# Six heads' decay masks from one interleaved table of powers, read in one transfer ahead of the second pair's q

## The chip, the cores and the metric

The kernel runs on one core of a Trainium2 chip. The metric is device time in microseconds (us). Three runs of the kernel before took 605.57, 605.16 and 603.69 us; their median is 605.16 us.

## What is computed

Three blocks follow each other: a linear attention whose weights decay with distance, a token- and channel-mixing MLP, and a two-dimensional Fourier mixing with a second MLP. The change lies in the first block. Batch is 2, with 8 heads, 768 positions and 64 values a head, all in float32. The decay of head h is the number `lam[h]`, between 0.97 and 0.99.

```python
rel = pos[:, None] - pos[None, :]
Dmask = np.where(rel >= 0, lam[:, None, None] ** rel[None, :, :], 0.0)
lam_pow = lam[:, None, None] ** (pos[None, :, None] + 1)
...
intra = np.einsum('bhic,bhjc->bhij', qb, kb) * Dmask[None]
intra = np.einsum('bhij,bhjd->bhid', intra, vb)
inter = np.einsum('bhid,bhde->bhie', qb * lam_pow[None], kv_state)
out[:, :, sl] = intra + inter
```

## The kernel before, in words

The kernel cuts the sequence into NC = 6 blocks of C = 128 positions and takes the heads two at a time: a pair (b, hp) is batch b and heads 2hp and 2hp + 1. There are eight pairs, numbered 0 to 7 as 4b + hp.

For each pair, `load_kp` (L400) brings the transposed keys into one of four slots of the tile `kp`, and `load_qkv` (L394) brings q, and then k and v in one transfer, into a tile `qkv`. `attention_scores` multiplies keys with queries on TensorE (L417). VectorE multiplies the scores by the head's decay mask on their way out of PSUM (L420: for each head one multiply of 4 blocks, 512 elements, and one of 2 blocks, 256 elements). GpSimd scales q by the powers of the decay (L424). `attention_states` scales the keys on ScalarE (L438, with the last column of the mask), forms the block updates on TensorE (L444) and chains them on VectorE (L448, L450). `attention_out` copies the states on ScalarE (L462), and TensorE adds both parts of the result (L468, L471), which ScalarE copies to `xT` (L473).

The masks lie in the tile `att` as `dT`, one 128 x 128 square per head. Each is a Toeplitz square: row p is a row of powers, shifted by p places. `attention_setup` makes them in two ways.

Heads 0 and 1 (the near heads, for pairs 0 and 4) are built on VectorE from the identity `ident` by seven doubling steps (L359, L374); the powers of lam that these steps need come from GpSimd (L371), from `lam_bc`, a copy of lam on all partitions.

Heads 2 to 7 (the far heads) come by way of memory. `pw8` has one head per partition and 256 places: 127 zeros, a one, and 128 powers, made by seven doubling multiplies on VectorE (L341). SP writes it to `scratch` in device memory (L344). The function `skew` (L348) reads it back, 128 rows per head, each one float further on than the last. `skew(2, 6)` stands behind pair 1's loads and fetches four heads, `skew(6, H)` stands behind pair 2's loads and fetches two (L1027).

GpSimd clears `bd` in `att` (L361), and makes the powers `pw` that scale q (L388) once the near masks are built.

The orders of SP and TensorE are written out by hand, in the order of the calls; those of VectorE, ScalarE and GpSimd come from a scheduler. The string `EARLY` (L37) gives the order of the front part: s for scores, u for states, r for the result of a pair, w for 8 warm-up transposes, l for loads, c and d for conversions of weights, x, h and o for the token mixing. 22 warm-up transposes (L1048) stand ahead of it; they read `ident`. The conversions turn 64-bit words into floats on ScalarE and VectorE (L231, L254 to L259); a raw weight tile can be loaded only once an earlier one has been converted, and SP issues in order. So raw_a_0, the first weight tile of the channel MLP, and behind it pair 7's loads, go out when VectorE has finished the last word operation (L259) of a token-mixing tile.

Of the kernel before, what the change touches and what calls it, by code (L numbers as in the profile page):

```python
# [25 lines left out]
P = 128  # L26
C = 128
# [35 lines left out]
def body(ctx: ExitStack, tc: tile.TileContext, qkv, kT, lam, w_tok1, w_tok2,  # L63
# [259 lines left out]
    def attention_setup():  # L323

        pw8 = temp(2 * C, "pw8")[:H]
        nc.sync.dma_start(pw8[:, C:C + 1], lam.rearrange("(h o) -> h o", o=1))
        lam_bc = sm_p.tile([P, H], F32, name="lam_bc")
        nc.scalar.dma_start(lam_bc, lam.rearrange("(o h) -> o h", o=1).broadcast_to([P, H]))
        kp = big_tile("kp").rearrange("p (i s) -> p i s", i=4)[:, :, :S]
        kps = [kp[:, i, :].rearrange("p (c j) -> p c j", j=C) for i in range(4)]  # L330
        load_kp(0, 0, kps[0])
        t = half_tile([P, 4, S], "qkv_0_0")
        for i in range(3):
            nc.sync.dma_start(t[:, i, :], qkv[0, 0, :, i])
        load_kp(0, 1, kps[1])
        nc.vector.memset(pw8[:, 0:C - 1], 0.0)
        nc.vector.memset(pw8[:, C - 1:C], 1.0)
        n = 1
        while n < C:
            w = min(n, C - n)  # L340
            ts(out=pw8[:, C + n:C + n + w], in0=pw8[:, C:C + w], scalar1=pw8[:, C + n - 1:C + n], scalar2=None,  # L341
               op0=ALU.mult)
            n *= 2
        nc.sync.dma_start(scratch, pw8)  # L344
        att = big_tile("att")
        dT = att[:, 0:H * C].rearrange("p (h j) -> p h j", h=H)

        def skew(h0, h1):  # L348
            src = bass.AP(scratch.tensor, scratch.offset + h0 * 2 * C, [[1, P], [2 * C, h1 - h0], [1, C]])
            nc.sync.dma_start(dT[:, h0:h1, :], src)  # L350

        load_qkv(0, 1)
        skew(2, 6)

# [9 lines left out]
        while n < C:  # L364
# [7 lines left out]
            for h in range(2):  # L372
                src = bands[i % 2][:, h]
                built = stt(out=dT[:, h, :] if 2 * n == C else bands[1 - i % 2][:, h, C // 2:],  # L374
                            in0=src[:, C // 2 - n:C // 2 - n + C], scalar=by[:, h:h + 1], in1=src[:, C // 2:],
                            op0=ALU.mult, op1=ALU.add).ins
# [15 lines left out]
        return dT, pw, kps, [bd[:, i] for i in range(2)], skew  # L392

    def load_qkv(b, hp):  # L394
        t = half_tile([P, 4, S], f"qkv_{b}_{hp}")
        nc.sync.dma_start(t[:, 0, :], qkv[b, hp, :, 0])
# [8 lines left out]
    def attention_scores(b, hp, dT, pw, kp):  # L405
# [5 lines left out]
        for g, cs in enumerate((range(4), range(4, NC))):  # L411
# [6 lines left out]
            for a in range(2):  # L418
                st = st2[:, a] if g else temp(4 * C, f"st_{n}_{a}").rearrange("p (c j) -> p c j", c=4)
                tt(out=st, in0=ps[a][:, :m * C].rearrange("p (c j) -> p c j", c=m),  # L420
                   in1=dT[:, 2 * hp + a:2 * hp + a + 1, :].to_broadcast([P, m, C]), op=ALU.mult)
# [7 lines left out]
    def attention_states(b, hp, dT, pw):  # L429
# [6 lines left out]
        with tc.issue_after(on_act[behind]):  # L436
            for a in range(2):
                on_act["keys", NP * b + hp] = nc.scalar.activation(  # L438
                    kn[:, :NC - 1, a * D:(a + 1) * D], kn[:, :NC - 1, a * D:(a + 1) * D], AF.Copy,
                    scale=dT[:, 2 * hp + a, C - 1:C]).ins  # L440
# [578 lines left out]
    with tc.manual_schedule(engines={ENG.SP, ENG.PE}):  # L1019
        dT, pw, kps, bds, skew = attention_setup()  # L1020
# [6 lines left out]
        skew(6, H)  # L1027
# [178 lines left out]
```

## Time and profile before

| what | value |
|---|---|
| median of three runs | 605.16 us |
| profiled execution | 605.05 us |
| its span | 603.1 us |
| TensorE matmul busy | 585.0 us, 97% |
| VectorE busy | 410.4 us, 68% |
| ScalarE busy | 269.9 us, 45% |
| GpSimd busy | 138.8 us, 23% |
| mean transfer rate | 109 GB/s |

The profiled execution is one run of the program; its span reaches from the first to the last instruction, and 1.95 us lie around it. Busy times are averages over stages with different limits, so a stage is read by itself: `PE` is TensorE's matmul, `PEld` its weight load, `DVE` VectorE, `ACT` ScalarE, `POOL` GpSimd, `SP` the engine that issues most transfers, and a q behind an engine's name its instruction queue. In a row of the timeline the bracket at the end gives the idle time just before it and what ended that wait.

### The profile page before, as it was taken

The numbers are of one execution on the slowest core, as the hardware profiler recorded it, in microseconds if no ns is written. First come the engines' busy times: TensorE is split into PE (matmuls) and PEld (weight loads), VectorE is DVE, ScalarE is ACT, GpSimd is POOL, SyncE is SP. The second block draws the span as 40 slices with busy tenths as digits, with TensorE's granted clock in tenths as the row PEclk, the third lists the DMA queues.
The fourth block names the chain that finished last, engine by engine and source line by source line (L and its number), as shares of the span: only waits on it lengthen the run. The fifth ranks groups of instructions, "written<-read, shape, count | busy, mean of one in ns | idle before, by whom it ended". The sixth has DMA issues, their size and how long they took to land. (4 is left out here: it accounts for less than half of the span.)

```text
span 603.1 us, 9588 instructions
## 1 busy us (share of the span) xinstructions
PE 585.0 (97%) x3704; PEld 545.9 (91%) x3704; DVE 410.4 (68%) x768; ACT 269.9 (45%) x536; POOL 138.8 (23%) x119
## 2 busy tenths in 40 slices
PE   8789999999999999999999999999999999999997
PEld 7777899999999999999989899899899888999886
DVE  6788893474586656848796896768775765664435
ACT  2756981255475555534454451324533434431110
POOL 5252331023230041101364110013501213120000
PEclk9999999999999999999999999999999999999999
DMA  7964431014448767410232000002521232200005
GB/s 275 407 261 158 185 122 60 0 71 141 137 148 265 245 192 219 146 64 2 57 101 71 19 2 35 18 1 58 168 88 36 88 122 88 87 2 1 0 1 209
DMA packets 24637, 65.58 MB, mean 109 GB/s; under 512 B 2824, under 2 KB 3984, under 8 KB 24592
## 3 DMA queue, kind: packets, MB, share of 16 engines
q1 hardware_dynamic: 24304, 64.83, 32.1%
q8 instruction: 29, 0.48, 0.3%
q10 hardware_dynamic: 288, 0.14, 0.1%
q14 instruction: 16, 0.13, 0.1%
HBM read 54.99 MB, written 9.97 MB: 108 GB/s over the span
## 5 line engine op out<-in xcount | busy, mean ns | idle before, releaser
L526 DVE SCALAR_TENSOR_TENSOR hid<-ph,hid 128x384 fp32r<-128x384 f32 x68 | 37.6, 553 | 59.6 <-ACT hid L525 59.4
L145 PE MATMUL ac<-w_b,hid 128*128 128x512 f32 x192 | 75.8, 395 | 0.0
L144 PE MATMUL ac<-w_b,hid 128*128 128x512 f32 x192 | 75.7, 394 | 0.0
L143 PE MATMUL ac<-w_b,hid 128*128 128x512 f32 x192 | 74.9, 390 | 0.0
L143 PE MATMUL ph<-uh,w_a 128*128 128x384 f32 x192 | 64.7, 337 | 0.0
L143 PE MATMUL ac<-hid,w_b 128*128 128x384 f32 x192 | 64.5, 336 | 0.0
L144 PE MATMUL ac<-hid,w_b 128*128 128x384 f32 x192 | 64.3, 335 | 0.0
L145 PE MATMUL ph<-uh,w_a 128*128 128x384 f32 x192 | 64.2, 335 | 0.0
L145 PE MATMUL ac<-hid,w_b 128*128 128x384 f32 x192 | 64.2, 334 | 0.0
L144 PE MATMUL ph<-uh,w_a 128*128 128x384 f32 x192 | 64.2, 334 | 0.0
L525 ACT ACTIVATE hid<-ph 128x384 fp32r<-128x384 f32 x68 | 33.1, 487 | 69.3 <-PE ph L145 68.9
L287 POOL TENSOR_TENSOR w_a<-m_a,w_a 128x512 fp32r<-128x512 f32 x18 | 25.5, 1418 | 131.9 <-ACT w_a L286 131.9
L145 PEld LDWEIGHTS ac<-w_b,hid 128*128 128x128 f32 x192 | 36.0, 188 | 7.7
L144 PEld LDWEIGHTS ac<-w_b,hid 128*128 128x128 f32 x192 | 36.0, 188 | 6.1
L143 PEld LDWEIGHTS ac<-w_b,hid 128*128 128x128 f32 x192 | 36.1, 188 | 5.8
L287 POOL TENSOR_TENSOR w_b<-m_b,w_b 128x512 fp32r<-128x512 f32 x18 | 25.3, 1403 | 49.6 <-ACT w_b L286 32.4
L143 PEld LDWEIGHTS ph<-uh,w_a 128*128 128x128 f32 x192 | 36.1, 188 | 0.4 <-issue 0.2
L144 PEld LDWEIGHTS ac<-hid,w_b 128*128 128x128 f32 x192 | 36.1, 188 | 0.3 <-DVE hid L526 0.3
L144 PEld LDWEIGHTS ph<-uh,w_a 128*128 128x128 f32 x192 | 36.1, 188 | 0.1
L143 PEld LDWEIGHTS ac<-hid,w_b 128*128 128x128 f32 x192 | 36.1, 188 | 0.0
L145 PEld LDWEIGHTS ph<-uh,w_a 128*128 128x128 f32 x192 | 36.0, 188 | 0.0
L145 PEld LDWEIGHTS ac<-hid,w_b 128*128 128x128 f32 x192 | 36.0, 188 | 0.0
(504 smaller groups left out, 1467.0 us busy)
## 6 DMA issues: line engine op xcount, KB each, us to landing
qkv<-qkv SPq DMA_DIRECT2D x7, 768.0 KB, 10.0
single_scratch<-m_a SPq DMA_DIRECT2D x16, 256.0 KB, 4.4
qkv<-qkv SPq DMA_DIRECT2D x10, 384.0 KB, 5.9
kp<-kT SPq DMA_DIRECT2D x8, 384.0 KB, 6.9
out<-u SPq DMA_DIRECT2D x11, 256.0 KB, 2.1
single_scratch<-m_b SPq DMA_DIRECT2D x10, 256.0 KB, 5.3
raw_t_0d<-w_tok SPq DMA_DIRECT2D x2, 384.0 KB, 9.3
raw_t_1d<-w_tok SPq DMA_DIRECT2D x2, 384.0 KB, 2.9
```

The lines of the kernel that those rows point to most:

```text
L143: nc.tensor.matmul(ps, wt[0], xt[0], start=first, stop=False, **kw)
L144: nc.tensor.matmul(ps, wt[0], xt[1], start=False, stop=False, **kw)
L145: nc.tensor.matmul(ps, wt[1], xt[0], start=False, stop=last, **kw)
L287: nc.gpsimd.tensor_tensor(out=t[:, 1, :n], in0=src, in1=f32(t[:, 0, :n]), op=ALU.subtract)
L525: mark("act", nc.scalar.activation(hi, ps, AF.Relu))
L526: mark("dve", stt(out=lo, in0=ps, scalar=0.0, in1=f32(hi), op0=ALU.max, op1=ALU.subtract))
```

## The change

One row of powers takes the place of `pw8`. It lies on one partition, in the part of `kp` that pairs 2 and 3 use later, and the six far heads stand side by side: place x holds the six heads' values for x. The seven doublings become tensor multiplies with 6 to 384 elements on that one partition. SP writes the row, 1,536 floats, to `scratch`, and one transfer reads it back as 128 rows of 768 floats, each 6 floats further on. In `att` the six far masks are then interleaved: the elements of one head's mask lie 6 floats (24 bytes) apart. The near heads' masks stay as they were.

SP's order changes: the scratch write now stands ahead of k and v of pair 0, and the read of all six far masks ahead of pair 1's q. Both `skew` calls go.

```diff
     def attention_setup():
 
-        pw8 = temp(2 * C, "pw8")[:H]
-        nc.sync.dma_start(pw8[:, C:C + 1], lam.rearrange("(h o) -> h o", o=1))
+        kp = big_tile("kp").rearrange("p (i s) -> p i s", i=4)[:, :, :S]
+        kps = [kp[:, i, :].rearrange("p (c j) -> p c j", j=C) for i in range(4)]
+
+
+        n_far = H - 2
+        powers = kp[0:1, 2:4, :].rearrange("o i s -> o (i s)").rearrange("o (x h) -> o x h", h=n_far)
+        nc.sync.dma_start(powers[:, C:C + 1, :], lam[2:H].rearrange("(o x h) -> o x h", o=1, x=1))
         lam_bc = sm_p.tile([P, H], F32, name="lam_bc")
         nc.scalar.dma_start(lam_bc, lam.rearrange("(o h) -> o h", o=1).broadcast_to([P, H]))
-        kp = big_tile("kp").rearrange("p (i s) -> p i s", i=4)[:, :, :S]
-        kps = [kp[:, i, :].rearrange("p (c j) -> p c j", j=C) for i in range(4)]
         load_kp(0, 0, kps[0])
         t = half_tile([P, 4, S], "qkv_0_0")
-        for i in range(3):
-            nc.sync.dma_start(t[:, i, :], qkv[0, 0, :, i])
-        load_kp(0, 1, kps[1])
-        nc.vector.memset(pw8[:, 0:C - 1], 0.0)
-        nc.vector.memset(pw8[:, C - 1:C], 1.0)
+        nc.sync.dma_start(t[:, 0, :], qkv[0, 0, :, 0])
+        nc.vector.memset(powers[:, 0:C - 1, :], 0.0)
+        nc.vector.memset(powers[:, C - 1:C, :], 1.0)
         n = 1
         while n < C:
             w = min(n, C - n)
-            ts(out=pw8[:, C + n:C + n + w], in0=pw8[:, C:C + w], scalar1=pw8[:, C + n - 1:C + n], scalar2=None,
-               op0=ALU.mult)
+            tt(out=powers[:, C + n:C + n + w, :], in0=powers[:, C:C + w, :],
+               in1=powers[:, C + n - 1:C + n, :].to_broadcast([1, w, n_far]), op=ALU.mult)
             n *= 2
-        nc.sync.dma_start(scratch, pw8)
+        nc.sync.dma_start(scratch.rearrange("(o n) -> o n", o=1), powers.rearrange("o x h -> o (x h)"))
+        for i in range(1, 3):
+            nc.sync.dma_start(t[:, i, :], qkv[0, 0, :, i])
         att = big_tile("att")
-        dT = att[:, 0:H * C].rearrange("p (h j) -> p h j", h=H)
-
-        def skew(h0, h1):
-            src = bass.AP(scratch.tensor, scratch.offset + h0 * 2 * C, [[1, P], [2 * C, h1 - h0], [1, C]])
-            nc.sync.dma_start(dT[:, h0:h1, :], src)
-
-        load_qkv(0, 1)
-        skew(2, 6)
+        far = att[:, 2 * C:H * C].rearrange("p (j h) -> p j h", h=n_far)
+        dT = [att[:, h * C:(h + 1) * C] for h in range(2)] + [far[:, :, h] for h in range(n_far)]
+
+        def far_masks():
+            nc.sync.dma_start(att[:, 2 * C:H * C], bass.AP(scratch.tensor, scratch.offset, [[n_far, P], [1, n_far * C]]))
+
+        load_kp(0, 1, kps[1])
+        load_qkv(0, 1, far_masks)
...
-    def load_qkv(b, hp):
+    def load_qkv(b, hp, first=lambda: None):
         t = half_tile([P, 4, S], f"qkv_{b}_{hp}")
+        first()
         nc.sync.dma_start(t[:, 0, :], qkv[b, hp, :, 0])
...
-                   in1=dT[:, 2 * hp + a:2 * hp + a + 1, :].to_broadcast([P, m, C]), op=ALU.mult)
+                   in1=dT[2 * hp + a].rearrange("p (o j) -> p o j", o=1).to_broadcast([P, m, C]), op=ALU.mult)
...
-                    scale=dT[:, 2 * hp + a, C - 1:C]).ins
+                    scale=dT[2 * hp + a][:, C - 1:C]).ins
...
-        skew(6, H)
```

SP's queue at the start of the program, before. `qkv_0_1` is pair 1, `qkv_0_2` pair 2; `att` holds the masks, and 128x768 is one of kp, q, k or v of a pair.

```order
L326 DMA pw8_101<-lam 8x1
L401 DMA kp_105<-kT 128x768
L334 DMA qkv_0_0_107<-qkv 128x768 x3
L401 DMA kp_105<-kT 128x768
L344 DMA pw_scratch<-pw8_101 8x256
L396 DMA qkv_0_1_123<-qkv 128x768
L397 DMA qkv_0_1_123<-qkv 128x1536
L350 DMA att_122<-pw_scratch 128x4x128
L401 DMA kp_105<-kT 128x768
L396 DMA qkv_0_2_165<-qkv 128x768
L397 DMA qkv_0_2_165<-qkv 128x1536
L350 DMA att_122<-pw_scratch 128x2x128
```

The same stretch of SP's queue in the changed kernel:

```order
L331 DMA kp_101<-lam 1x6
L405 DMA kp_101<-kT 128x768
L336 DMA qkv_0_0_106<-qkv 128x768
L345 DMA pw_scratch<-kp_101 1x1536
L347 DMA qkv_0_0_106<-qkv 128x768 x2
L405 DMA kp_101<-kT 128x768
L353 DMA att_120<-pw_scratch 128x768
L400 DMA qkv_0_1_122<-qkv 128x768
L401 DMA qkv_0_1_122<-qkv 128x1536
L405 DMA kp_101<-kT 128x768
L400 DMA qkv_0_2_164<-qkv 128x768
L401 DMA qkv_0_2_164<-qkv 128x1536
```

The scratch write has moved ahead of three transfers (k and v of pair 0 and the keys of pair 1), the read of the masks ahead of pair 1's q, k and v, and the second read is gone.

GpSimd's queue after the program's constants, before. `ident` is the identity that the warm-up reads; the memset of `att` clears the states' place.

```order
masks.py:197 MEMSET ident 128x128
masks.py:199 ISA
masks.py:199 AFFINE_SELECT ident<-ident 128x128
L361 MEMSET att 128x1280
L371 TENSOR_TENSOR lp<-lam_bc 128x2
```

And in the changed kernel:

```order
masks.py:197 MEMSET ident 128x128
L364 MEMSET att 128x1280
masks.py:199 ISA
masks.py:199 AFFINE_SELECT ident<-ident 128x128
L374 TENSOR_TENSOR lp<-lam_bc 128x2
```

The memset of `att` has moved ahead of the step that completes `ident`. VectorE, ScalarE and TensorE keep their orders; on VectorE the memsets and doublings of the new row of powers stand where those of `pw8` stood.

## Rows read from the trace of the kernel before

**Rows 1.** The page: span and number of instructions.

```profile
span 603.1 us, 9588 instructions
```

**Rows 2.** Busy time by stretches of 5 us: engines, granted clock, transfer share, GB/s.

```profile
40.00:45.00 5.00, 3.61 (x55) 2.94 (x52) 4.96 (x11) 2.12 (x5) 1.46 (x2) 1.00 0.25 72
...
75.00:80.00 5.00, 5.00 (x30) 5.00 (x30) 4.98 (x7) 3.16 (x7) 1.72 (x2) 1.00 0.35 110
```

**Rows 3.** Timeline, VectorE, 0 to 45 us: start, duration, instruction, idle before it.

```profile
2.16 1.76 DVE L341 TENSOR_SCALAR pw<-pw 8x1 f32<-8x1 f32 x7 [0.83 <-DMA pw<-lam]
...
15.34 1.95 DVE L420 TENSOR_TENSOR st<-s,att 128x512 f32<-128x512 f32 x4 [3.23 <-DMA att<-pw_scratch]
...
21.26 0.23 DVE L448 COPY state<-u 128x64 f32<-128x64 f32 x1 [0.65 <-PE u L444]
...
24.75 1.95 DVE L420 TENSOR_TENSOR st<-s,att 128x512 f32<-128x512 f32 x4 [2.00 <-PE s L417]
...
28.01 0.76 DVE L256 TENSOR_SCALAR m_t<-m_t 128x512 uint32<-128x512 uint32 x2
```

**Rows 4.** Timeline, SP's queue, 0 to 45 us.

```profile
3.96 0.30 SPq L344 DMA_DIRECT2D pw_scratch<-pw  x1
...
9.09 0.38 SPq L350 DMA_DIRECT2D att<-pw_scratch  x1
```

**Rows 5.** Busy time by stretches of 1 us; the last number is GB/s.

```profile
10.00:11.00 1.00, 1.00 (x13) 0.83 (x13) 0.36 (x3) 0.00 (x0) 0.84 (x3) 1.00 0.99 412
11.00:12.00 1.00, 1.00 (x24) 1.00 (x20) 0.89 (x4) 0.62 (x2) 1.00 (x1) 1.00 0.66 216
...
13.00:14.00 1.00, 1.00 (x24) 1.00 (x22) 0.00 (x0) 0.00 (x0) 0.98 (x1) 1.00 0.90 256
```

**Rows 6.** Timeline, ScalarE, 0 to 45 us.

```profile
19.36 1.01 ACT L438 ACTIVATE qkv<-qkv,att 128x320 f32<-128x320 f32 x2 [2.26 <-DMA qkv<-qkv]
```

**Rows 7.** Timeline, GpSimd, 0 to 45 us.

```profile
1.01 0.29 POOL masks.py:199 TENSOR_SCALAR_AFFINE_SELECT ident<-ident 128x128 f32<-128x128 f32 x1
1.25 1.17 POOL L361 MEMSET att<- 128x1280 f32 x1
```

**Rows 8.** Timeline, TensorE, 0 to 45 us.

```profile
1.36 4.59 PE L1048 MATMUL warm<-ident 128*128 128x128 f32 x22 [1.36 <-POOL ident masks.py:199]
6.33 1.61 PE L417 MATMUL s<-qkv,kp 64*128 64x128 f32 x24 [0.39 <-DMA qkv<-qkv]
...
10.65 1.61 PE L417 MATMUL s<-qkv,kp 64*128 64x128 f32 x24
```

**Rows 9.** Groups of VectorE, forms apart: count, busy us, mean ns, idle before.

```profile
L420 DVE TENSOR_TENSOR st<-s,att 128x512 f32<-128x512 f32 x16 | 10.3, 682 | 5.3 <-DMA att<-pw_scratch 3.2 <-PE s L417 2.0
...
L420 DVE TENSOR_TENSOR st<-s,att 128x256 f32<-128x256 f32 x16 | 5.9, 412 | 0.0
...
L257 DVE SCALAR_TENSOR_TENSOR m_t<-raw_t_0d,m_t 128x384 uint32<-128x384 uint32 x2 | 1.1, 548 | 0.0
```

**Rows 10.** Groups of ScalarE, forms apart.

```profile
L286 ACT ACTIVATE w_b<-m_b 128x512 fp32r<-128x512 f32 x18 | 11.4, 633 | 11.0 <-DVE m_b L259 11.0
...
L779 ACT ACTIVATE gr<-xT 128x512 f32<-128x512 f32 x4 | 4.5, 1152 | 0.0
```

**Rows 11.** Timeline, VectorE, 38 to 80 us.

```profile
42.78 1.94 DVE L420 TENSOR_TENSOR st<-s,att 128x512 f32<-128x512 f32 x4
...
46.87 1.95 DVE L420 TENSOR_TENSOR st<-s,att 128x512 f32<-128x512 f32 x4
49.47 1.89 DVE L139 TENSOR_TENSOR x<-px,x 128x512 fp32r<-128x512 f32 x3 [0.65 <-ACT x L138]
```

**Rows 12.** Timeline, SP's queue, 38 to 90 us.

```profile
53.36 0.33 SPq L211 DMA_DIRECT2D raw_a_0d<-w_ch  x1
```

**Rows 13.** Waits of SP's queue, 50 to 58 us: us in total, times, longest.

```profile
SPq L211 <- DVE m_t L259: 7.1, 2, 6.1
```

**Rows 14.** Timeline, TensorE, 38 to 90 us.

```profile
60.26 1.61 PE L417 MATMUL s<-qkv,kp 64*128 64x128 f32 x24 [0.32 <-DMA qkv<-qkv]
```

More of the change, by code (lines that the diff above doesn't have):

```diff
@@ L373, in attention_setup @@
                 src = bands[i % 2][:, h]
-                built = stt(out=dT[:, h, :] if 2 * n == C else bands[1 - i % 2][:, h, C // 2:],
+                built = stt(out=dT[h] if 2 * n == C else bands[1 - i % 2][:, h, C // 2:],
                             in0=src[:, C // 2 - n:C // 2 - n + C], scalar=by[:, h:h + 1], in1=src[:, C // 2:],
@@ L391, in attention_setup @@
         pair[0, 0] = t
-        return dT, pw, kps, [bd[:, i] for i in range(2)], skew
-    def load_qkv(b, hp):
+        return dT, pw, kps, [bd[:, i] for i in range(2)]
+    def load_qkv(b, hp, first=lambda: None):
         t = half_tile([P, 4, S], f"qkv_{b}_{hp}")
+        first()
         nc.sync.dma_start(t[:, 0, :], qkv[b, hp, :, 0])
@@ L1019, in body @@
     with tc.manual_schedule(engines={ENG.SP, ENG.PE}):
-        dT, pw, kps, bds, skew = attention_setup()
+        dT, pw, kps, bds = attention_setup()
         def load(n):
@@ L1196 @@
     out = nc.dram_tensor("out", (B, 6, P, DM), F32, kind="ExternalOutput").ap()
-    scratch = nc.dram_tensor("pw_scratch", (H, 2 * C), F32, kind="Internal").ap()
+    scratch = nc.dram_tensor("pw_scratch", ((H - 2) * 2 * C,), F32, kind="Internal").ap()
     singles = nc.dram_tensor("single_scratch", (2 * F2 // P, P, 512), F32, kind="Internal").ap()
```

## The prediction

> **What bounds the kernel now.** The profiled execution took 605.05 us for a span of 603.1 us [rows 1], so 1.95 us lie around it; it stands 0.11 us under the median of 605.16 us. About 0.3% (1.8 us) is what a measurement of this kernel can tell from no change. I read busy time by stage first: from 75 us on TensorE is busy in all of a stretch, while from 40 to 45 us VectorE is busy 4.96 of 5 us and TensorE only 3.61 [rows 2]. The change touches only what runs before about 70 us. What it wins or loses there is handed to a TensorE that has no idle time left to absorb it, so the time moves by the moment at which the front part ends. Three limits rule the front part.
>
> First the transfers. VectorE waits 3.23 us, to 15.34 us, for the masks of pair 1, the longest wait of its early timeline [rows 3]. SP issues that read at 9.09 us, although it had issued the write it depends on at 3.96 us [rows 4]. That write sits behind the loads issued before it: lam, kp 0, the three parts of pair 0, kp 1. Then the loads bind again: the keys of pair 2 start at 19.36 us, after ScalarE waited 2.26 us for pair 2's load [rows 6].
>
> Second, from 28.01 us on [rows 3], VectorE's own queue. The multiply of pair 5's scores follows at 42.78, that of pair 6 at 46.87, and the only gap before the next step is 0.65 us, at 49.47 [rows 11].
>
> Third, SP issues raw_a_0 only at 53.36 us, after up to 6.1 us of waiting for VectorE's L259, and pair 7's kp and qkv stand behind it in SP's queue [rows 12, 13]. TensorE's scores of pair 7 start at 60.26 us after a wait for that load [rows 14]. A microsecond on VectorE between 28 and 53 us is therefore a microsecond at 60 us.
>
> **The powers.** Seven scalings take 1.76 us from 2.16 us on [rows 3]. They become seven tensor multiplies of 6 to 384 elements on one partition, 762 in all. VectorE's rate on contiguous operands follows from the two forms of the score multiply: (682 - 412)/256 = 1.05 ns an element, and 142 ns fixed [rows 9]. So 0.8 us is added, and the chain ends near 4.7 us in place of 3.9. The larger memset (762 elements, 0.8 us) lies in the 0.83 us in which VectorE waits for lam [rows 3]; without that cover it would cost the same again. The two near heads' masks, pair 0's score multiply and GpSimd's power chain behind them all come 0.8 us later. They are not yet late: pair 1's scores wait for their q (below).
>
> **GpSimd.** Its memset of att now lies ahead of ident's select. It takes 1.17 us and the select ended near 1.30 us [rows 7], so the 22 warm-up matmuls (4.59 us) start at 2.5 instead of 1.36 us, and pair 0's scores at 7.1 instead of 6.33 [rows 8]. The next wait, pair 1's q, hides this too.
>
> **The transfers.** The scratch write goes out at about 4.8 us with only kp 0 and q 0 ahead of it, lands near 7 us, and the far masks are read then, 2 us earlier than the first mask read was. The price: k and v of pair 0 and kp 1 wait on SP for the powers, which leaves the transfer engines idle some 0.7 us between the end of q 0 and the data of k 0. In return the stretch after the first mask read disappears: 412 GB/s at 10 to 11 us, then 216 to 256 for three microseconds [rows 5], which is some 0.5 MB or 1.3 us lost on a read in 512 rows of 512 bytes. All six far masks now are 128 rows of 3,072 bytes, 0.39 MB: 0.95 us at the full rate, 1.6 us at that slow rate; I take 1.1, nearer the full rate, since the rows are as long as those of the loads. The last third of the masks now also precedes pair 2 (0.3 us). Net, pair 2's load lands 0 to 1.7 us sooner; I take 1.0.
>
> Pair 1's q now follows the masks and lands near 12 us, so pair 1's scores start at 12.0 rather than 10.65 us [rows 8], and its multiply near 13.1 rather than 15.34. After that TensorE's order (result of pair 0, states of pair 1, scores of pair 2, states of pair 2, result of pair 1, scores of pair 3) runs into pair 2's load again. So most of the 2.2 us won by the masks is lost there, and pair 3's multiply could start at 23.7 rather than 24.75 us: 1.05 us won, between 0 and 1.7.
>
> **The strided masks.** Head h's mask was 128 neighbouring floats; now its elements lie 24 bytes apart. Six of the eight pairs use it (pairs 1, 2, 3, 5, 6, 7), each in two multiplies of 512 and two of 256 elements. No VectorE instruction of the trace reads at such a step. Bound below: L257 reads words 8 bytes apart and takes 548 ns for 384 elements [rows 9], which is 142 + 384 x 1.05 = 545: no cost. Bound above: L779 is a ScalarE copy whose source elements lie exactly 24 bytes apart (every sixth float, read backwards). It takes 1,152 ns where a contiguous 512-element copy takes 633 [rows 10], 1.0 ns more an element. I take the upper row, since its step is the very one, and the memory read is the same. Two ways of carrying it over to the 1,536 elements of a pair differ a little: at ScalarE's strided rate of about 1.88 ns an element VectorE loses 0.83 ns, 1.3 us a pair; at half VectorE's own rate 1.05 ns, 1.6 us. I take 1.4 us a pair, with 0 to 1.6 for the range.
>
> [...]
>
> **The sum at the places that bind.** Pair 1's and pair 2's extra 1.4 us each fall before the wait for pair 2's load and its states (0.65 us of idle even now [rows 3]) and cost nothing. Pair 3's counts: -1.05 + 1.4 = +0.35 us where the word operations begin (28.01 us before). Pair 4 uses contiguous masks. Pairs 5 and 6 add 2.8 us, less the 0.65 us gap [rows 11]: +2.15. Raw_a_0, pair 7's load and the scores at 60.26 us come 2.5 us later. Pair 7's own 1.4 us lies beside TensorE work that has some slack; I take +0.3, between 0 and 1.0. Together +2.8: **607.9 us**. Break-even would be near 0.5 us a pair: pair 3 and pairs 5 and 6 make three times the price, less 0.65 and 1.05.
>
> **The rivals.** *One, faster than before:* VectorE reads the 24-byte step at its normal rate, as ScalarE's slowdown may be ScalarE's own or come from reading backwards. Then only the transfer gain is left, -1.0 us: 604.0 us, between 603.3 and 605. For it speaks the 8-byte row, against it the 24-byte one. It decides below 0.5 us a pair, which is a 512-element multiply under about 850 ns.
>
> *Two, the transfers win nothing:* the scratch write from one partition lands late, or reading one small region of memory 128 times is the real slowness at 11 to 14 us, whatever the row length. Then pair 2's load lands no sooner, pair 3's multiply starts no earlier, and the strided cost stands alone: +1.3 at 28 us, +2.15, +0.3: 608.8 us, up to 609.6 if pair 7 pays its full 1.0. For it: three microseconds at a low rate began just as that region was read. Against it: the rows now are six times longer and the write's queue is shorter.
>
> **How the numbers follow.** Forecast 0.58, with its own range of 606.6 to 609.6 (transfer gain 1.7 to 0, 1.3 to 1.6 us a pair, pair 7 from 0 to 1.0; all the bad ends together would give 610.2); rival one 0.26; rival two 0.16. Slower by over 0.3% means above 606.97 us: 0.46 of the forecast, 0.14 of rival two, 0.01 of rival one, 0.61 together. Faster means under 603.34: 0.07, all from rival one. The rest, 0.32, is no change. The range of 603.6 to 609.6 holds nearly all of the forecast, most of rival one and of rival two. The predicted time is the forecast's 607.9.
>
> **What would show it.** Right, if the score multiplies of the far pairs last about 1.1 us (512 elements) and 0.63 us (256) while pairs 0 and 4 stay at 682 and 412 ns; if pair 1's multiply starts near 13 us; if the word operations start within a microsecond of 28 us; and if raw_a_0 goes out near 56 us and pair 7's scores start near 62.8. If the far multiplies stay at 682 ns, rival one holds. If pair 1's multiply does not start before 15 us, or 200 to 250 GB/s still stand behind the mask read, rival two does. I would be wrong outright if TensorE showed idle time past 75 us, or if the front part lost time to something not named here, such as a late near mask.

## The result, and the profile after

| kernel | median | range of the runs | to the kernel before |
|---|---|---|---|
| before | 605.64 us | 603.69 to 606.81, 6 runs | 1 |
| changed | 609.27 us | 608.41 to 610.33, 6 runs | 1.0063, 95% interval 1.0046 to 1.0081 |

The change costs 0.63%. The direction and the mechanism were forecast. The forecast time was 1.4 us too low (0.5 us of it because the median before, over six runs, is 605.64 us and not 605.16), and the parts of the sum were off by more than their sum shows.

The page of the changed kernel first: the span is 3.8 us longer than in [rows 1].

```profile
span 606.9 us, 9581 instructions
```

The groups of VectorE, forms apart. All 16 multiplies of a form share a line, so the mean mixes 12 strided and 4 contiguous ones: (16 x 980 - 4 x 682) / 12 = 1,079 ns for 512 elements, and (16 x 571 - 4 x 412) / 12 = 624 ns for 256, against 682 and 412 in [rows 9].

```profile
L424 DVE TENSOR_TENSOR st<-s,att 128x512 f32<-128x512 f32 x16 | 15.1, 980 | 3.8 <-PE s L421 3.7
L424 DVE TENSOR_TENSOR st<-s,att 128x256 f32<-128x256 f32 x16 | 8.4, 571 | 0.0
```

VectorE's timeline. The four multiplies of a pair in a row take 1.95 us for pair 0 and 3.07 to 3.21 us for the far pairs 1, 2, 3, 5 and 6: about 1.17 us more a pair, where the prediction took 1.4. Pair 1's multiply starts at 15.28 us, as before (15.34 in [rows 3]), and now waits for scores in place of masks.

```profile
1.94 2.12 DVE L342 TENSOR_TENSOR kp<-kp 1x6 f32<-1x6 f32 x7
...
8.30 1.95 DVE L424 TENSOR_TENSOR st<-s,att 128x512 f32<-128x512 f32 x4
...
15.28 3.12 DVE L424 TENSOR_TENSOR st<-s,att 128x512 f32<-128x512 f32 x4 [3.03 <-PE s L421]
...
25.53 3.10 DVE L424 TENSOR_TENSOR st<-s,att 128x512 f32<-128x512 f32 x4 [0.69 <-PE s L421]
...
29.95 0.75 DVE L256 TENSOR_SCALAR m_t<-m_t 128x512 uint32<-128x512 uint32 x2
...
43.37 3.07 DVE L424 TENSOR_TENSOR st<-s,att 128x512 f32<-128x512 f32 x4
...
51.69 1.90 DVE L139 TENSOR_TENSOR x<-px,x 128x512 fp32r<-128x512 f32 x3
```

SP's queue: the write goes out at 4.09 us, and the read that waits for it at 6.11 us. ScalarE's timeline: the keys of pair 2 wait until 20.14 us, 0.78 us later than in [rows 6].

```profile
4.09 0.25 SPq L345 DMA_DIRECT2D pw_scratch<-kp  x1
...
6.11 0.33 SPq L353 DMA_DIRECT2D att<-pw_scratch  x1
...
55.60 0.33 SPq L211 DMA_DIRECT2D raw_a_0d<-w_ch  x1
```

```profile
20.14 1.01 ACT L442 ACTIVATE qkv<-qkv,att 128x320 f32<-128x320 f32 x2 [1.33 <-DMA qkv<-qkv]
```

The stretches of 1 us (the last number is GB/s) show why. The slow stretch that stood behind the first mask read at 11 to 14 us in [rows 5] has moved along with the read, to 9 to 12 us, and it is no shallower, although each piece of the read is now 3,072 bytes.

```profile
9.00:10.00 1.00, 0.94 (x18) 0.73 (x18) 1.00 (x3) 0.00 (x0) 0.77 (x4) 1.00 0.73 92
10.00:11.00 1.00, 1.00 (x20) 0.93 (x16) 0.48 (x2) 0.00 (x0) 0.91 (x2) 1.00 0.81 230
11.00:12.00 1.00, 0.43 (x4) 0.19 (x2) 0.87 (x4) 0.61 (x2) 0.94 (x1) 1.00 0.97 304
```

TensorE's timeline, the rows with waits that matter. The scores of pair 7 come 1.84 us later than in [rows 14], and a wait for VectorE stands at 74.79 us, where the kernel before has none.

```profile
2.42 4.56 PE L1051 MATMUL warm<-ident 128*128 128x128 f32 x22 [2.42 <-POOL ident masks.py:199]
6.91 1.61 PE L421 MATMUL s<-qkv,kp 64*128 64x128 f32 x24
...
14.12 1.61 PE L421 MATMUL s<-qkv,kp 64*128 64x128 f32 x24 [2.68 <-issue]
...
62.10 1.61 PE L421 MATMUL s<-qkv,kp 64*128 64x128 f32 x24
...
74.79 0.45 PE L143 MATMUL ht<-w_t,h1s 128*128 128x384 f32 x1 [1.32 <-DVE xT L520]
```

The stretches of 5 us around that wait (busy times of TensorE, its weight load, VectorE, ScalarE and GpSimd):

```profile
70.00:75.00 5.00, 3.68 (x20) 3.34 (x20) 5.00 (x11) 4.08 (x10) 2.07 (x2) 1.00 0.28 105
75.00:80.00 5.00, 5.00 (x58) 4.57 (x58) 4.77 (x10) 4.95 (x11) 1.11 (x1) 1.00 0.32 105
```

From 75 us on TensorE is again busy 5.00 of 5 us, as in [rows 2]. So the 3.8 us are lost before that, and the place of the loss can be read along the rows: +1.94 us where the word operations begin (28.01 to 29.95), +0.59 at pair 5's multiply (42.78 to 43.37), +2.22 at L139 (49.47 to 51.69), +2.24 at raw_a_0 (53.36 to 55.60), and 3.8 at the end, of which 1.56 us therefore arise behind raw_a_0.

### The profile page after: what moved, and what is told of

Its sections match the earlier page's. It is cut to its first block, busy times and chain, and to the rows that moved or that the text cites. A ratio compares the mean times of both kernels' runs of the same rounds, so it can differ in the third digit from the quotient of the medians.

```text
span 606.9 us, 9581 instructions
## 1 busy us (share of the span) xinstructions
PE 584.3 (96%) x3704; PEld 545.5 (90%) x3704; DVE 418.4 (69%) x768; ACT 270.1 (45%) x536; POOL 138.9 (23%) x119
## 5 line engine op out<-in xcount | busy, mean ns | idle before, releaser
L143 PE MATMUL ac<-w_b,hid 128*128 128x512 f32 x192 | 74.9, 390 | 0.0
L143 PE MATMUL ph<-uh,w_a 128*128 128x384 f32 x192 | 64.7, 337 | 0.0
L143 PE MATMUL ac<-hid,w_b 128*128 128x384 f32 x192 | 64.4, 336 | 0.0
L287 POOL TENSOR_TENSOR w_a<-m_a,w_a 128x512 fp32r<-128x512 f32 x18 | 25.2, 1397 | 134.1 <-ACT w_a L286 134.1
L143 PEld LDWEIGHTS ac<-w_b,hid 128*128 128x128 f32 x192 | 36.1, 188 | 5.8
L287 POOL TENSOR_TENSOR w_b<-m_b,w_b 128x512 fp32r<-128x512 f32 x18 | 25.3, 1407 | 50.0 <-ACT w_b L286 35.9
L143 PEld LDWEIGHTS ph<-uh,w_a 128*128 128x128 f32 x192 | 36.1, 188 | 0.4 <-issue 0.2
L143 PEld LDWEIGHTS ac<-hid,w_b 128*128 128x128 f32 x192 | 36.1, 188 | 0.0
```

Of the source, the lines that this page charges most:

```text
L143: nc.tensor.matmul(ps, wt[0], xt[0], start=first, stop=False, **kw)
L287: nc.gpsimd.tensor_tensor(out=t[:, 1, :n], in0=src, in1=f32(t[:, 0, :n]), op=ALU.subtract)
```

## The experiments

The runs were made in four sets, each beside the kernel before on the same chip (medians of before 605.67, 605.47, 605.12 and 605.05 us; a ratio is always to the kernel before in its own set).

### Step and order, apart

The change does two things at once: it puts the heads side by side (a step of 24 bytes for VectorE) and it moves the mask read ahead of pair 1's q. One run keeps the new order and goes back to a step of 4 bytes:

```diff
-        powers = kp[0:1, 2:4, :]....rearrange("o (x h) -> o x h", h=n_far)
+        powers = kp[0:1, 2:4, :]....rearrange("o (h x) -> o h x", h=n_far)
...
-            nc.sync.dma_start(att[:, 2 * C:H * C], bass.AP(scratch.tensor, scratch.offset, [[n_far, P], [1, n_far * C]]))
+            nc.sync.dma_start(far, bass.AP(scratch.tensor, scratch.offset, [[1, P], [2 * C, n_far], [1, C]]))
```

> The changed kernel with each far head's mask contiguous again: the row of powers lies head by head, and the one read in the new place of the queue takes 128 rows of 6 pieces of 512 bytes. Order of all queues as in the changed kernel. Theory 1 (the 24-byte step on VectorE is what costs): the far pairs' 512-element multiplies return from 1.10 to 0.68 us, the word operations begin near 28.8 us instead of 29.95, raw_a_0 goes out near 53.4 instead of 55.60, and the time is 605.5 to 606.5 us. Theory 2 (the new order of the transfers is what costs): the multiplies return to 0.68 us all the same, but pair 2's load still comes late and the time stays at 608 to 609 us.

Measured: 606.05 us, ratio 1.0003 (0.9991 to 1.0016), in theory one's range, and the 512-element multiplies take 682 ns again. But its front was late for a reason of its own. Lambda now lay in six pieces of 4 bytes 1,024 bytes apart, and the powers waited for it; VectorE's timeline:

```profile
3.69 2.03 DVE L342 TENSOR_TENSOR kp<-kp 1x6 f32<-1x6 f32 x7 [1.69 <-DMA kp<-lam]
```

So it was run again with lambda loaded as one piece of 24 bytes and copied into place by VectorE. This is the clean-order run below.

```diff
+        lam_far = sm_p.tile([1, n_far], F32, name="lam_far")
-        nc.sync.dma_start(powers[:, :, C:C + 1], lam[2:H]...)
+        nc.sync.dma_start(lam_far, lam[2:H].rearrange("(o h) -> o h", o=1))
...
+        nc.vector.tensor_copy(powers[:, :, C:C + 1], lam_far.rearrange("o (h x) -> o h x", x=1))
```

> The changed order of the transfers (one read of 128 rows of masks ahead of pair 1's q) with each head's powers side by side, so that VectorE reads the masks at a step of 4 bytes; lambda comes in one contiguous piece into a tile of its own, since in the run before this one its six separate pieces landed 1.75 us late and blurred the front. Values as the changed kernel's. Theory one (the step of 24 bytes is the cost; the new order by itself costs what the mask read's slow stretch costs, some 0.4 to 1.0 us): pair 1's multiply at about 15.3 and 1.95 us long, the wordwise operations at 29.95 - 1.17 = 28.8, median 605.3 to 606.6. Theory two (the new order gains 1 us, as the prediction had it, and the late lambda hid that in the run before): pair 1's multiply at about 13.1, the wordwise operations at about 27, median 604.0 to 604.8. Theory three (the new order costs most of the loss): median 607 or more.

Measured: 605.61 us, ratio 0.9998 (0.9988 to 1.0008). VectorE's timeline, SP's queue and TensorE's timeline of this run:

```profile
15.42 1.95 DVE L426 TENSOR_TENSOR st<-s,att 128x512 f32<-128x512 f32 x4 [2.74 <-PE s L423]
...
30.12 0.75 DVE L256 TENSOR_SCALAR m_t<-m_t 128x512 uint32<-128x512 uint32 x2
```

```profile
53.91 0.33 SPq L211 DMA_DIRECT2D raw_a_0d<-w_ch  x1
```

```profile
14.05 2.25 PE L423 MATMUL s<-qkv,kp 64*128 64x128 f32 x24 [2.90 <-issue]
```

The new order wins nothing, as theory one said: pair 1's multiply at 15.42 us and not at 13.1. It also loses nothing that can be measured, which theory one had put at 0.4 to 1.0 us; by the interval it could be up to 0.5. The word operations begin 2.1 us late, and raw_a_0 goes out only 0.55 us late. So between 28 and 43 us a late start is mostly made up again.

Part of that late start is TensorE's clock in this one execution. TensorE had waited 2.90 us before pair 1's scores, and the granted clock of the microseconds from 14 to 19 us was 0.92, 0.50, 0.50, 0.50 and 0.88 (1.00 is the full clock); the changed kernel's profile has 1.00 there. The scores took 2.25 us in place of 1.61, and from their start to pair 1's states 5.60 us went by in place of the changed kernel's 3.99. At the full clock the word operations would have begun near 28.5 us (an estimate: 30.12 less these 1.6), close to theory one's 28.8. The mean clock of the whole program is under 0.999 in 11 of this run's 12 executions, in 5 of 6 of the changed kernel and in 15 of 26 of the kernel before in this run's set, so the new order seems to bring such a stretch about more often. No run was made for it.

The third cell is the step with the order of before:

```diff
-        nc.sync.dma_start(t[:, 0, :], qkv[0, 0, :, 0])
+        for i in range(3):
+            nc.sync.dma_start(t[:, i, :], qkv[0, 0, :, i])
+        load_kp(0, 1, kps[1])
...
-        load_kp(0, 1, kps[1])
-        load_qkv(0, 1, far_masks)
+        load_qkv(0, 1)
+        far_masks()
```

> The changed kernel with its interleaved masks and its single read, but SP's order as before: k and v of pair 0 and kp 1 ahead of the scratch write, the mask read behind pair 1's q, k and v. Theory 1 (the step costs): the far multiplies stay at 1.10 us, pairs 5 and 6 still add 1.7 us before raw_a_0, and the time is 608 to 609.5 us. Theory 2 (the order costs): the time returns to 605.5 to 606.5 us although the multiplies are slow.

Measured: 608.28 us, ratio 1.0043 (1.0028 to 1.0058), as theory one said. With it the four cells are: 4 bytes and old order 1; 4 bytes and new order 0.9998; 24 bytes and old order 1.0043; both 1.0063. The step costs 2.6 us in the old order and 3.9 us in the new one. So the step is what makes the kernel slower. The new order costs nothing measurable by itself; whether it adds something beside the step (609.27 against 608.28 us) stays open, since those two intervals overlap.

### What a step costs

> As the run beside it, but the masks of the six far heads are read at steps of 4, 8, 12, 16, 20 and 24 bytes by pairs 1, 2, 3, and of -4, -24, -8, -12, 16 and 16 bytes by pairs 5, 6, 7: their values are wrong, the amount of work is the same. It gives the time of one 512-element multiply for each step, which no other run does. [...] Theory two (the cost grows with the step): 0.76 to 0.85 at 8 bytes, about 0.95 at 16, 1.10 at 24. Theory three (any step but 4 costs the same): 1.10 already at 8 bytes.

```diff
+        flat = att[:, 2 * C:H * C]
+        def step(s):
+            s_ = flat[:, 0:(C - 1) * abs(s) + 1:abs(s)]
+            return s_ if s > 0 else s_[:, ::-1]
...
+        dT = {0: near + [step(s) for s in (1, 2, 3, 4, 5, 6)],
+              1: near + [step(s) for s in (-1, -6, -2, -3, 4, 4)]}
```

VectorE's timeline of this run (one execution), single multiplies of 512 elements; the steps are, from top to bottom, 8, 12, 16, 20, -24 and -12 bytes. A step of 24 bytes has 1,079 ns in the changed kernel.

```profile
16.54 0.68 DVE L435 TENSOR_TENSOR st<-s,att 128x512 f32<-128x512 f32 x1
...
22.04 0.87 DVE L435 TENSOR_TENSOR st<-s,att 128x512 f32<-128x512 f32 x1
...
22.83 1.12 DVE L435 TENSOR_TENSOR st<-s,att 128x512 f32<-128x512 f32 x1
...
26.38 1.07 DVE L435 TENSOR_TENSOR st<-s,att 128x512 f32<-128x512 f32 x1
...
44.21 1.04 DVE L435 TENSOR_TENSOR st<-s,att 128x512 f32<-128x512 f32 x1
...
48.84 0.86 DVE L435 TENSOR_TENSOR st<-s,att 128x512 f32<-128x512 f32 x1
```

A step of 8 bytes is free (0.68 us, as at 4 bytes); 12 cost 0.19 us a multiply; 16, 20 and 24 cost 0.36 to 0.44 and no longer grow; the sign makes no difference beyond 0.04 us (0.87 and 0.86 at 12 bytes, 1.08 and 1.04 at 24). Theory two's 0.76 at 8 bytes did not come, and its growth with the step ends at 16; theory three fails at 8. So the row of [rows 10] was the right one to carry over for its step. Its reading backwards need not have slowed it, since backwards cost VectorE nothing; ScalarE was not tried. Why the cost is there at 12 bytes and no longer grows from 16 on, no run shows.

### What slows the transfers

Two runs of the changed kernel change the mask read alone: every row from the same address, so that no row starts at an odd place, and rows from 128 separate places of an input.

```diff
-            nc.sync.dma_start(att[:, 2 * C:H * C], bass.AP(scratch.tensor, scratch.offset, [[n_far, P], [1, n_far * C]]))
+            nc.sync.dma_start(att[:, 2 * C:H * C], bass.AP(scratch.tensor, scratch.offset, [[0, P], [1, n_far * C]]))
```

> The changed kernel, but all 128 rows of the mask read start at the same address of the scratch (no shift from row to row; the masks are not the reference's). If the slow stretch behind the read comes from many reads of one small region, it stays: under 250 GB/s for about two microseconds after 9 us, pair 1's scores near 14.1 us. If it comes from rows that begin 24 bytes apart and so off any alignment, it goes: 380 to 430 GB/s throughout, pair 1's scores near 12.5 us.

```diff
-            nc.sync.dma_start(att[:, 2 * C:H * C], bass.AP(scratch.tensor, scratch.offset, [[n_far, P], [1, n_far * C]]))
+            nc.sync.dma_start(att[:, 2 * C:H * C], kT[1, 0])
```

> The changed kernel, but the mask read takes the same 128 rows of 3,072 bytes from 0.39 MB of an input, no two rows overlapping (the masks are not the reference's). If the small region is what slows the transfers, the rate stays at 380 to 430 GB/s behind the read, pair 1's scores start near 12.5 us instead of 14.12, pair 2's load lands 0.8 to 1.5 us sooner and the time is about 1 us less than the changed kernel's. If the loss comes from the place in the queue (SP's wait, the gap before k of pair 0), the low rate after 9 us stays and nothing moves.

Measured, one run each: 608.99 us and 607.23 us. The stretches of the first, then of the second:

```profile
9.00:10.00 1.00, 1.00 (x24) 0.79 (x22) 1.00 (x3) 0.00 (x0) 0.76 (x4) 1.00 0.78 132
10.00:11.00 1.00, 1.00 (x12) 0.86 (x8) 0.38 (x2) 0.00 (x0) 0.90 (x2) 1.00 0.91 212
11.00:12.00 1.00, 0.12 (x2) 0.00 (x0) 0.88 (x4) 0.61 (x2) 0.94 (x1) 1.00 0.94 283
```

```profile
9.00:10.00 1.00, 1.00 (x24) 0.93 (x24) 1.00 (x3) 0.00 (x0) 0.77 (x4) 1.00 0.90 273
10.00:11.00 1.00, 0.80 (x8) 0.56 (x6) 0.38 (x2) 0.00 (x0) 0.91 (x2) 1.00 1.04 396
11.00:12.00 1.00, 0.00 (x0) 0.00 (x0) 0.87 (x4) 0.62 (x2) 0.93 (x1) 1.00 1.08 402
```

In the first the slow stretch stays, with pair 1's scores at 14.00 us, so odd starts are not its cause. In the second the same bytes in the same number of pieces, from the same place in the queue, cost a short dip (307 GB/s at 8 us, 273 at 9) and then come at 396 and 402 GB/s. Pair 1's multiply then starts at 13.86 us and the word operations at 28.68, which is the front that the prediction had described; the one time of 607.23 us is 1.2 us under the lowest run of the changed kernel. But this run changes more than the size of the region: its rows come from an input and not from memory written 2 us earlier, and the read goes out 0.4 us sooner, at 5.71 us, since it need not wait for the write. Next the length of the pieces, tried with the two heads of a pair side by side (a free step of 8 bytes) and pieces of 1,024 bytes:

```diff
+        powers = kp[0:1, 2:4, :]....rearrange("o (g x a) -> o g x a", g=3, a=2)
...
+            nc.sync.dma_start(far, bass.AP(scratch.tensor, scratch.offset, [[2, P], [4 * C, 3], [1, 2 * C]]))
```

> The powers of two heads of a pair stand side by side, so that VectorE reads the masks at a step of 8 bytes and one transfer brings 128 rows of three pieces of 1,024 B, in the changed kernel's place in the order; lambda comes in one contiguous piece. Values as the changed kernel's. The multiply of 512 elements should take 0.68 us, as the step of 8 bytes did in the run with the six steps. Theory one (many reads of one small region slow the transfers, whatever the length of a piece): a stretch of 90 to 250 KB/us stays between 9 and 12 us, pair 1's multiply at 15 or later, median 605.2 to 606.0, as the clean order had. Theory two (the 768 pieces of 512 B slow them): no such stretch, multiply at 14 or sooner, median 604.0 to 605.0.

Measured: 605.46 us, ratio 1.0004 (0.9991 to 1.0017), and the slow stretch stays: 122, 253 and 292 GB/s from 9 to 12 us. The multiplies take 682 ns, so the step of 8 bytes is free here too. Pieces of 512 (199 GB/s at the lowest, in the clean-order run), 1,024 and 3,072 bytes are all slow from the 6 KB of `scratch`; pieces of 3,072 bytes from an input are not. So the length of a piece is not the cause, and theory two falls. What it is about that memory, that it is small, read many times over or newly written, these runs do not tell apart.

### What pair 7 pays

Once out of the changed kernel, once into the clean-order kernel:

```diff
+        dT += [att[:, h * C:(h + 1) * C] for h in range(6, 8)]
...
-                   in1=dT[2 * hp + a]....to_broadcast([P, m, C]), op=ALU.mult)
+                   in1=dT[2 * hp + a + (2 if b and hp == 3 else 0)]....to_broadcast([P, m, C]), op=ALU.mult)
```

> The changed kernel, but pair 7's two masks are read at a step of 4 bytes from two other blocks of the same tile (its mask values are wrong, nothing else changes). Theory one (the step's cost in pair 7 lies almost whole on TensorE's path, as the idle times of 0.46 and 1.32 us behind pair 7's matmuls suggest): both idle times go, 1.7 to 2.0 us less than the changed kernel, median 607.2 to 607.8. Theory two (the prediction's term: pair 7 costs 0.3 us and the pairs before it 2.5): median 608.7 to 609.2.

The second, beside the same change of `in1`:

```diff
+        flat = att[:, 2 * C:H * C].rearrange("p (j h) -> p j h", h=n_far)
+        dT += [flat[:, :, h] for h in range(4, 6)]
```

> The clean-order kernel (step of 4 bytes everywhere, 605.61 us), with pair 7 alone reading its two masks at a step of 24 bytes from the same tile (its mask values are wrong, nothing else changes). Theory one (VectorE is full while pair 7 is worked on, so that its own 1.3 us of lengthening lies whole on the path): 1.1 to 1.5 us more, median 606.7 to 607.1. Theory two (the prediction's term of 0.3 us): median 605.7 to 606.1. Theory three (1.8 us, as read from TensorE's idle times in the changed kernel): 607.2 to 607.6.

Measured: 608.17 us, ratio 1.0044 (1.0029 to 1.0059), 1.1 us under the changed kernel; and 606.10 us, ratio 1.0018 (1.0009 to 1.0028). The second median stands where theory two put it, but the kernel before ran 0.35 us faster in this set than in that of the clean order: by the ratios the step in pair 7 costs 1.2 us, and against the run with pairs side by side, in the same set and with the same multiplies (605.46), 0.6 us. By the intervals each of these differences is known to about 0.9 us only, so they hardly exclude the prediction's 0.3. The first run's time lies between its two theories. The wait that the step brings is the one at L143; TensorE's timeline of the second run, whose clean-order twin does not have it:

```profile
72.44 0.44 PE L143 MATMUL ht<-w_t,h1s 128*128 128x384 f32 x1 [1.37 <-DVE xT L524]
```

The 0.46 us that ended by ScalarE at 68.40 us in the changed kernel, which the first expectation counted in, is not the step's: the clean-order run has 0.49 us in the same place. The time between raw_a_0 and the end says more. Without a step in pair 7 it is 549.7 us before (603.1 - 53.36), 549.9 in the clean-order run and 549.1 with pairs side by side; with the step of 24 bytes it is 551.3 in the changed kernel, 551.1 with the old order, and 550.6 where pair 7 alone is strided. These put pair 7 at 0.7 to 2.2 us, 1.4 between the means. The run with pair 7 alone contiguous has 550.7 and does not fit; its profiled execution was its slowest, with a load late by 1.40 us at pair 7. So pair 7 costs more than the 0.3 of the prediction and near 1 us; the size stays open.

Its own multiplies are not all of it. In the changed kernel a word operation of VectorE stands in the queue behind them:

```profile
72.45 1.63 DVE L259 SCALAR_TENSOR_TENSOR m_a<-raw_a_1d,m_a 128x512 uint32<-128x512 uint32 x1
```

It began while GpSimd's multiply L287 ran, from 71.65 to 73.54 us, and ended 0.54 us after it. In the kernel before it started at 68.50 us, just ahead of that multiply (68.58), and took 0.68 us. The runs with a 24-byte step in pair 7 have the long one, 1.62 to 1.65 us in the changed kernel, with the old order and with pair 7 alone strided; the others mentioned here have the short one. So the lengthened multiplies bring the word operation behind GpSimd's multiply in place of ahead of it, and some 0.95 us of VectorE's full stretch from 70 to 75 us is that wait.

### Versions that might beat both

If a small region is slow, sixteen copies of the powers should help. The first version computes them on 16 partitions, at a step of 4 bytes, with six reads:

```diff
+        n_far, K = H - 2, 16
+        powers = kp[0:K, 2:4, :]....rearrange("o (h x) -> o h x", h=n_far)
+        lam_far = sm_p.tile([K, n_far], F32, name="lam_far")
+        nc.sync.dma_start(lam_far, lam[2:H].rearrange("(o h) -> o h", o=1).broadcast_to([K, n_far]))
...
+        def far_masks(hp):
+            for h in range(2 * hp - 2, 2 * hp):
+                src = bass.AP(scratch.tensor, scratch.offset + h * 2 * C, [[n_far * 2 * C + P // K, K], [1, P // K], [1, C]])
+                nc.sync.dma_start(far[:, h, :], src)
```

> Step of 4 bytes, and the powers computed on 16 partitions and written as 16 copies, of which each serves 8 rows of the read; the masks of heads 2 and 3 are read ahead of pair 1's q, those of pairs 2 and 3 ahead of their pairs' q, six transfers of 128 rows x 512 B. Values as the changed kernel's. Theory one (many reads of one small region slow every transfer beside them): no stretch under 230 KB in 1 us between 9 and 13 us, pair 1's multiply at 12.5 to 13.9, pair 2's keys before 19.0, median 603.6 to 604.8, under the kernel before. Theory two (the number of small rows slows the transfers, wherever they lie): a stretch of 90 to 230 KB/us stays, the multiply at 14.5 or later, median 605.3 to 606.6.

Measured: 605.60 us, ratio 1.0005 (0.9992 to 1.0018). Between 9 and 13 us the rates are 399, 361, 311 and 335 GB/s, but behind the third pair of reads, which goes out at 15.37 us, the microsecond from 16 us has 213. So the copies made the stretch shallower and did not end it. Lambda in 16 pieces lands 1.7 us later, the write goes out at 5.93 us, and pair 1's multiply starts at 17.52. By its numbers theory two came out (a multiply at 14.5 or later, the median in its range), but the front was late before the read began, and the profiled execution was the slowest of the twelve (608.53 us), with the granted clock at 0.50 in parts of 15 to 19 and 35 to 39 us. It does not decide between the theories. The second version writes the one partition's powers to sixteen places, at a step of 8 bytes:

```diff
+        nc.sync.dma_start(scratch..., powers....to_broadcast([1, K, n_far * 2 * C]))
...
+        def far_masks(g):
+            src = bass.AP(scratch.tensor, scratch.offset + g * 4 * C, [[n_far * 2 * C + 2 * P // K, K], [2, P // K], [1, 2 * C]])
+            nc.sync.dma_start(far[:, g], src)
```

> As the run beside it, a step of 8 bytes, but the write sends the one partition's powers to sixteen places, each copy serves 8 rows of the read, and the masks come pair by pair, each pair's 128 rows of 1,024 B ahead of its q. Values as the changed kernel's. Theory one (a spread region reads at the full rate, and writing the copies is cheap): no stretch under 250 KB/us after the write has landed, pair 1's multiply at 12.5 to 14.0, median 603.6 to 604.9, under the kernel before. Theory two (what the reads gain, the sixteenfold write from one partition and its wait give back): the write lands 1 us or more later than the 2 us that it took in the changed kernel, pair 1's multiply at 15 or later, median 605.3 to 606.8.

Measured: 607.32 us, ratio 1.0031 (1.0017 to 1.0044), slower than both theories' ranges. Theory two's other numbers hold: the read that waits for the write goes out 5.4 us after it in place of 2.0, and pair 1's multiply starts at 16.11 us (the granted clock was 0.50 from 13 to 16 us). Its profiled execution (605.39 us) was its fastest, so the profile shows the loss in part only. The write goes out at 4.17 us and the read behind it at 9.57, and everything on SP's queue behind it waits. In its stretches, one whole microsecond moves nothing:

```profile
7.00:8.00 1.00, 1.00 (x19) 0.88 (x16) 1.00 (x5) 0.00 (x0) 0.00 (x0) 1.00 0.00 0
```

The last version keeps these copies and goes back to the order of before, with nothing behind the write that is needed soon:

```diff
+        for i in range(3):
+            nc.sync.dma_start(t[:, i, :], qkv[0, 0, :, i])
+        load_kp(0, 1, kps[1])
...
+        load_qkv(0, 1)
+        far_masks(0)
+        far_masks(1)
...
         load(2)
+        far_masks(2)
```

> The sixteen copies of the run before, at a step of 8 bytes, but with the transfers in the order of the kernel before: k and v of pair 0 and all of pair 1 ahead of the masks, so that nothing waits behind the slow sixteenfold write; pair 1's and pair 2's masks follow pair 1's load, pair 3's follow pair 2's load. Values as the changed kernel's. Theory one (only the wait behind the write held the copies back; reads of a spread region cost their bytes alone): no stretch without transfers before 9 us and none under 250 KB/us after it, pair 1's multiply at 13.5 to 15.3, the wordwise operations at 27.0 to 27.8, median 603.8 to 604.9, under the kernel before. Theory two (the sixteenfold write or the three reads by themselves slow the loads beside them): a slow stretch stays, the wordwise operations at 28 or later, median 605.0 to 606.5.

Measured: 603.92 us, ratio 0.9979 (0.9965 to 0.9993): 1.1 us under the kernel before, the only one of all that is under it by more than its interval. Its timeline of VectorE, its queue of SP and one of its stretches:

```profile
13.56 1.96 DVE L428 TENSOR_TENSOR st<-s,att 128x512 f32<-128x512 f32 x4 [1.23 <-DMA att<-pw_scratch]
...
29.65 0.76 DVE L256 TENSOR_SCALAR m_t<-m_t 128x512 uint32<-128x512 uint32 x2
```

```profile
52.80 0.33 SPq L211 DMA_DIRECT2D raw_a_0d<-w_ch  x1
```

```profile
12.00:13.00 1.00, 1.00 (x20) 0.88 (x19) 0.30 (x2) 0.67 (x3) 1.00 (x2) 1.00 1.11 249
```

Pair 1's multiply starts 1.8 us earlier than before and the time is in theory one's range, but two of that theory's numbers fail: a stretch of 249 and 243 GB/s stays at 12 to 14 us (and 226 at 18), and the word operations begin at 29.65 us, later than before. The rows that agree with the gain are pair 5's multiply at 42.21 us and raw_a_0, 0.57 and 0.56 us earlier: between the word operations and pair 5 VectorE waited behind a GpSimd multiply twice, and three times in the kernel before. That is where this execution caught up; that the copies brought it about is not shown. It is faster by 0.2%, less than the 0.3% that the prediction took for no change; why is not settled.

## Why the prediction was right, and where it was wrong

The side and the mechanism were right: the step of 24 bytes is what makes the kernel slower. The time of 609.27 us lies in the range, 1.4 us above the forecast and inside rival two's 608.8 to 609.6. That it came this near owes something to luck, since two terms were wrong, and one that was missing balanced most of what the first of them cost. By step:

- **The powers.** "0.8 us is added": the chain took 2.12 us in place of 1.76 and ended at 4.06 us, not 4.7. The write went out at 4.09 us and its read at 6.11 us, a little earlier than forecast. It gained nothing, because of the next step but one.
- **GpSimd.** Right: the warm-up began at 2.42 us (forecast 2.5) and pair 0's scores at 6.91 (7.1), and pair 1's q hid it.
- **The transfers: this step failed.** "I take 1.1, nearer the full rate, since the rows are as long as those of the loads." The length of a row was not the cause. The read from the 6 KB of `scratch` is slow at 512, 1,024 and 3,072 bytes (199, 122 and 92 GB/s at the lowest), and the read of as many bytes from an input much less so (273). Pair 2's keys came 0.78 us later in place of 1.0 us sooner, pair 3's multiply at 25.53 us in place of 23.7. This is rival two's mechanism, to which I gave 0.16; whether the smallness of the region does it stays open. The row that could have warned was there: in [rows 5] the rate fell just when that region was read, and no other row of 512-byte pieces was looked at to separate length from place.
- **The price of the step.** Right in kind, a little high: 1.17 us a pair for 1.4, and 1,079 and 624 ns for the forecast's 1.1 us and 0.63. Choosing the row with the very step over the row with the same engine was the decision that carried the forecast.
- **Pairs 1 and 2, put at nothing.** Nearly right: with the step and the old order, pair 3's multiply starts at 25.02 us, 0.27 us later than before.
- **Pairs 5 and 6.** "2.8 less the 0.65 gap: +2.15." Two pairs at 1.17 less 0.65 make 1.69; measured between pair 5's start and L139 2.22 - 0.59 = 1.63 us. The subtraction of the gap was right.
- **A term that was missing.** +1.94 us at 28 us was only +0.59 at 43 us. The prediction took a microsecond there for a microsecond later, since VectorE is busy 13.42 of the 15 us from 28 to 43 us in the kernel before. But in the rows here each word operation of VectorE that began while GpSimd ran a multiply ended behind it: 0.54 to 0.55 us after its end for L259 and 0.28 us for L256, with durations from 0.89 to 1.81 us. The later starts met GpSimd's multiplies nearer to their ends. VectorE's and GpSimd's timelines, two of the kernel before and two of the changed kernel:

```profile
33.70 1.81 DVE L259 SCALAR_TENSOR_TENSOR m_t<-raw_t_1d,m_t 128x512 uint32<-128x512 uint32 x1
...
38.86 1.60 DVE L256 TENSOR_SCALAR m_t<-m_t 128x512 uint32<-128x512 uint32 x1
```

```profile
33.42 1.54 POOL L424 TENSOR_TENSOR qkv<-qkv,att 128x640 f32<-128x640 f32 x1 [2.06 <-DMA qkv<-qkv]
...
38.64 1.54 POOL L424 TENSOR_TENSOR qkv<-qkv,att 128x640 f32<-128x640 f32 x1 [0.77 <-DMA qkv<-qkv]
```

```profile
35.64 1.25 DVE L259 SCALAR_TENSOR_TENSOR m_t<-raw_t_1d,m_t 128x512 uint32<-128x512 uint32 x1
...
40.15 0.89 DVE L256 TENSOR_SCALAR m_t<-m_t 128x512 uint32<-128x512 uint32 x1
```

```profile
34.80 1.55 POOL L428 TENSOR_TENSOR qkv<-qkv,att 128x640 f32<-128x640 f32 x1 [2.10 <-ACT w_t L286]
...
39.21 1.55 POOL L428 TENSOR_TENSOR qkv<-qkv,att 128x640 f32<-128x640 f32 x1
```

  The two word operations give back 0.56 + 0.71 = 1.27 of the 1.35 us. The clean-order run made up as much (2.1 to 0.55 us), so it is not the step's doing. No run changed GpSimd's work to test it. It happened to balance what the failed transfer step had cost, so that raw_a_0 came out at 55.60 us, near the forecast 56.
- **Pair 7: mis-sized.** "I take +0.3, between 0 and 1.0." Its own multiplies got 1.3 us longer (1.10 + 1.09 + 1.24 us against 0.69 + 0.68 + 0.75 in the clean-order run), and a word operation behind them got 0.95 us longer by the wait for GpSimd. VectorE is busy in all of 70 to 75 us, and TensorE waits 1.32 us at L143, for VectorE. Behind raw_a_0 the changed kernel lost 1.56 us. The slack seen on TensorE was no slack, since the work beside it waits for the same VectorE.

The sum as the two profiles give it: +0.59 at pair 5, +1.65 to raw_a_0, +1.56 behind it, 3.8 us of span.

## What to carry to other kernels

Before a layout saves a transfer, cost what it does to every later reader: a step of 8 bytes was free for 4-byte elements on VectorE (0.68 us for 512 of them), and at 16 to 24 bytes each element cost about 0.8 ns more (1,079 ns for 512 at 24), so two heads side by side were free and six were not. When a transfer is slow, separate the length of its pieces from the place they come from, by reading the same pieces elsewhere (here 92 GB/s at the lowest from `scratch` and 273 from an input). And gaps of the bounding engine need not be slack for an engine beside it: VectorE was busy 5.00 of 5 us from 70 to 75 us, and TensorE's gap of 1.32 us at L143 waited for it. Before comparing the start of a step in two profiles, compare the granted clock of the stretch ahead of it: 0.50 for three microseconds in the clean-order run, which by the estimate above put its word operations 1.6 us later.

## What the runs showed of the hardware that I had not expected

- Behind a read of 128 overlapping rows out of one newly written region of 6 KB the transfers fell to 92 to 304 GB/s for three microseconds in the changed kernel, against 378 to 430 from 12 to 20 us, and to 199 and 122 at the lowest with pieces of 512 and 1,024 bytes. Sixteen copies, in two orders, still had stretches of 213 and 226 GB/s.
- In the rows shown above, a word operation of VectorE that began while GpSimd ran a multiply ended 0.54 to 0.55 us (L259) or 0.28 us (L256) after that multiply, and counts as busy all that time: 1.81 us in place of 0.68 for one L259.
- A load of 24 bytes in six pieces of 4 bytes held its reader until 3.69 us, where the same bytes in one piece let it start at 1.94 (in the changed kernel).
- A write of one partition's 6 KB to sixteen places let its reader go 5.4 us after its issue, where the single write took 2.0.
